# Longformer attention and a feed-forward layer on one core: the steady part's transfers in one written order, the global probabilities turned on VectorE and exchanged through HBM

## The chip, the cores and the metric

The kernel runs on one core of a Trainium2 chip. The metric is the device time of one execution in microseconds (us), and the figure to compare is the median of several runs. One execution was also profiled; its trace gives the time of each instruction on TensorE (PE for matmuls, PEld for weight loads), VectorE (DVE), ScalarE (ACT), GpSimd (POOL) and the sync engine's queue of transfers (SPq).

## The reference

Eight batches of eight heads: 512 local tokens per head attend to a window of 32 tokens on each side and to 32 global tokens; the 32 global tokens attend to everything. The result goes, token by token, through a layer of 512 x 2048, a leaky bend with a slope for each hidden unit, and a layer of 2048 x 512.

```python
s_g = scale * np.matmul(q_g, k_all.transpose(0, 1, 3, 2))
out_g = np.matmul(sm(s_g), v_all)
mask = np.abs(pos[:, None] - pos[None, :]) <= window
s_ll = np.where(mask, s_ll, -1000000000.0)
s_l = np.concatenate([s_lg, s_ll], axis=-1)
out_l = np.matmul(sm(s_l), np.concatenate([v_g, v_l], axis=2))
...
h = x @ w_in
g = np.maximum(h, 0.0) + alpha * np.minimum(h, 0.0)
return (g @ w_out).astype(np.float32)
```

## The kernel before

**Units of work.** Heads are taken in 32 pairs (P, four pairs to a batch). The feed-forward layers are cut into 16 tiles of 128 hidden units. A step t is one such tile for one group of tokens: `f1(t)` is the first layer's twelve matmuls into a PSUM bank `h_ps`, `leak` and `bend` make `g`, `round_g` and `rest_g` split it into a high and a low part (`gh`, `gl`), and `f2` adds it to four output banks in two parts, two steps later (`LAG = 2`). Groups are the eight batches and, last, all global tokens: 144 steps.

**Local attention of a pair.** `local_scores` (PSUM `s_ps`, from `qk`), maxima and exponentials (`p`), then the exchange that turns the probabilities: VectorE transposes 32 x 32 blocks (`pb`), one DMA writes them to HBM, and four DMAs a head read them back in another order (`pt`, `local_exchange`, `give` and `take`). `local_values` multiplies `pt` with `vw` into `o_ps`; `local_weights` scales the result (`xq`) and sends it through the same kind of exchange (`xb`) into `x_raw`, the input of the next group's first layer.

**Global attention of two pairs** (index k, sixteen in all). `global_scores` (PSUM `g_ps`, from `gn`; two short memsets fill an unused corner first), exponentials into `sg_sb`, `global_transposes` (four TensorE transposes into PSUM `gt`, copied by ScalarE and VectorE into `sgt_sb`; a rest of 32 columns is turned by VectorE), `global_values` (`go`, from `sgt_sb` and `vg`) and `global_outputs` (`gx`).

**What sets the order.** TensorE follows the order in which the code is written throughout. The first part, up to step 18, is spelled out in the string `ORDER` (lines 37 to 50): a letter for a function and a number for its pair or step, and it fixes ScalarE and VectorE too. After it comes the loop over steps (line 612), in which `plan` (lines 536 to 553) hangs local work on every fourth step and global work on chosen steps, at the places "mid" (ahead of the second layer's first part) or "post" (between its two parts). There ScalarE, VectorE and GpSimd are ordered by a scheduler. Transfers on SP keep the written order up to line 578, where `dma.on = False` hands them to the scheduler; only inside `local_exchange` are they kept in order. SP is one queue: a transfer that waits for its data holds all behind it.

**Buffers.** `vw` and `qk` have one buffer each for pairs from 4 on, so that a load can start only when TensorE has finished with the pair before. `g`, `gh`, `gl`, `p`, `pb`, `pt`, `xq` and `xb` share 21 buffers of 128 x 512. `h_ps`, `o_ps` and `go` share two PSUM banks, `s_ps`, `g_ps`, `gt` and `gx` two others.

Of the kernel before, what the change touches and what calls it, by code (L numbers as in the profile page):

```python
# [8 lines left out]
F32 = mybir.dt.float32  # L9
# [8 lines left out]
NB, NH, SL, SG, D = 8, 8, 512, 32, 64  # L18
NPAIR = 4
# [24 lines left out]
    x4 H7 L8 C5 L7 j10 V5 r9 T6 N5 k11 A7 g9 u10 j11 C6 X5 B7 x5 S7 H9 l10 k12 L9 F10 h12 R7 u11  # L44
    s12 V6 r10 l11 E7 A8 N6 g10 B8 j12 H10 S8 h13 F11 L10 k13 R8 u12 X6 r11 A9 x6 l12 E8 g11 T7
    s13 B9 j13 F12 h14 s14 u13 A10 k14 l13 r12 B10 H11 g12 F13 h15 L11 j14 C7 V7 r13 g13 u14 A11
    N7 k15 l14 X7 B11 s15 x7 H13 F14 H12 j15 A12 L12 u15 r14 l15 B12 g14 F15 d8 e8 L13 A13 r15 H14
    g15 H15 B13 L15 L14 F16 r16 g16 H16 L16 A14 V8 S9 B14 N8 R9 F17 p9 r17 q9 g17 d9 A15 B15 e9 H17
    L17 F18 r18 g18 G0 H18 L18 A16 B16
"""  # L50
GROUPS = [("l", b) for b in range(NB)] + [("g", 0)]
# [33 lines left out]
def longformer_ffn(ctx: ExitStack, tc: tile.TileContext, qk, vs, gn, vg, w, alpha, out):  # L85
# [13 lines left out]
    beta_sb = const.tile([128, NF], F32, name="beta_sb")  # L99
    pick = const.tile([128, 64], F32, name="pick")  # L100
    og_sb = const.tile([128, 128], F32, name="og_sb")
    sgt_sb = const.tile([128, 5, 2, 64], F32, name="sgt_sb")
    x_raw = const.tile([128, NPAIR, SL], F32, name="x_raw")
    x_glb = const.tile([128, NPAIR, NB * SG], F32, name="x_glb")

# [2 lines left out]
    def matmul(*a, **k):  # L108
        return tc.keep_in_program_order(nc.tensor.matmul(*a, **k))  # L109

    def transpose(*a):
        return tc.keep_in_program_order(nc.tensor.transpose(*a))  # L112

    def stage(name, dtype=F32):
        return work.tile([128, 512], dtype, tag="st", name=name, bufs=NST)
# [4 lines left out]
    def copy(engine, dst, src):  # L120
        if engine == "a":
            act.copy(dst, src)
        else:
            vec.tensor_copy(dst, src)

    def bank(tag, name):
        return psum.tile([128, 512], F32, tag=tag, name=name, bufs=2 if tag in "hs" else 1)
# [91 lines left out]
    def load_v(P):  # L219
        if P < NPAIR:  # L220
            t = wpool.tile([128, 2048], F32, tag="w", name="vw")
        else:
            t = work.tile([128, 2048], F32, tag="v", name="vw", bufs=1)
        vws[P] = t.rearrange("k (e i d) -> k e i d", e=2, i=8)
        for e in range(2):
            off = (P * KS + 32 * e) * 128
            src = bass.AP(tensor=vs.tensor, offset=off, ap=[[128, 128], [96 * 128, 8], [1, 128]])
            dma.dma_start(vws[P][:, e], src)
# [35 lines left out]
    def local_exps(P, heads=(0, 1)):  # L264
        if 0 in heads:
            z_of[P] = small("z", 8)
        for h in heads:
            src, mn, scale = ps_of.pop((P, h))
            p = pr_of[P, h] = stage("p") if P < NRAW else pr_of[P, h]
            for i in range(4):  # L270
                k = 2 * i + h
                act.activation(p[:, 128 * i : 128 * i + 128], src[:, i], AF.Exp, bias=mn[:, i : i + 1], scale=scale, accum_out=z_of[P][:, k : k + 1])
        if 1 in heads:
            rz_of[P] = small("rz", 8)
            act.activation(rz_of[P], z_of.pop(P), AF.Copy, bias=1e-9)
# [23 lines left out]
            dma.dma_start(put[32 * b : 32 * b + 32].rearrange("k (w n) -> k w n", w=4), spread[:, b].rearrange("(w k) n -> k w n", w=4))  # L299

    def local_exchange(P, heads=(0, 1)):
        on, dma.on = dma.on, True
        for h in heads:
            ps_of[P, h] = give(pr_of.pop((P, h)), "pb")
        if 1 in heads:
            for h in range(2):
                pt_of[P, h] = stage("pt")
                take(pt_of[P, h], ps_of.pop((P, h)))
        dma.on = on

    xs = {}

# [43 lines left out]
        xh, xl = xs[0, P]  # L356
        vec.tensor_tensor(xl, ps_of.pop(P), xh.bitcast(F32), op=ALU.subtract)

    gns, vgs, sgs, gz = {}, {}, {}, {}
    big = []  # L360

    def load_gn(k):
        if not big:
            big.append(wpool.tile([128, 2048], F32, tag="w", name="gn"))
        for e in range(2):
            gns[2 * k + e] = big[0][:, 576 * e : 576 * e + 576]
            dma.dma_start(gns[2 * k + e], gn[2 * k + e])

    def load_vg(k):
        for P in (2 * k, 2 * k + 1):  # L370
            vgs[P] = wide("vg")[:, 0:640].rearrange("k (y d) -> k y d", y=5)
            dma.dma_start(vgs[P], vg[P])

    def global_scores(k):
        ss = [bank("s", "g_ps") for h in range(2)]
        for h in range(2):
            vec.memset(ss[h][64:128, 256:288], -3.0e38)
        for r, c0, n in ((0, 32, 288), (1, 320, 256)):
            for e in range(2):
                t = gns[2 * k + e]  # L380
                for h in range(2):
                    hs, q0 = slice(64 * h, 64 * h + 64), 64 * r + 32 * e
                    matmul(ss[h][q0 : q0 + 32, 0:n], t[hs, 0:32], t[hs, c0 : c0 + n], start=True, stop=True)
        for e in range(2):
            del gns[2 * k + e]
        m, z = small("gm", 4), small("gz", 16)
        sg_sb = sgs[k] = big[0][:, 1152:1728].rearrange("q (h n) -> q h n", h=2)
        for h in range(2):
            vec.tensor_reduce(m[:, h : h + 1], ss[h][:, 0:288], axis=AX.X, op=ALU.max)
        vec.tensor_scalar(m[:, 2:4], m[:, 0:2], -0.125, None, op0=ALU.mult)  # L390
        vec.tensor_copy(m[0:64, 0:2], m[64:128, 2:4])
        vec.tensor_tensor(m[0:64, 2:4], m[0:64, 2:4], m[0:64, 0:2], op=ALU.min)
        vec.tensor_copy(m[64:128, 2:4], m[0:64, 2:4])
        for h in range(2):
            act.activation(sg_sb[:, h], ss[h][:, 0:288], AF.Exp, bias=m[:, 2 + h : 3 + h], scale=0.125, accum_out=z[:, h : h + 1])
        vec.tensor_copy(z[0:64, 2:4], z[64:128, 0:2])
        vec.scalar_tensor_tensor(z[0:64, 2:4], z[0:64, 2:4], 1e-9, z[0:64, 0:2], op0=ALU.add, op1=ALU.add)
        vec.reciprocal(z[0:64, 2:4], z[0:64, 2:4])
        vec.tensor_copy(z[64:128, 2:4], z[0:64, 2:4])
        gz[k] = z  # L400

    def global_transposes(k):
        ps, sg_sb = bank("s", "gt"), sgs.pop(k)
        for h in range(2):
            for e in range(2):
                c = 256 * h + 128 * e
                transpose(ps[:, c : c + 128], sg_sb[:, h, 128 * e : 128 * e + 128], ident)
        for h in range(2):
            dst = sgt_sb[:, 0:4, h].rearrange("k (r e) n -> k r e n", r=2)
            copy("ad"[h], dst, ps[:, 256 * h : 256 * h + 256].rearrange("k (e r n) -> k r e n", e=2, r=2))  # L410
            for e in range(2):
                vec.transpose(sgt_sb[0:32, 4, h, 32 * e : 32 * e + 32], sg_sb[32 * e : 32 * e + 32, h, 256:288])

    def global_values(k):
        ps = bank("h", "go")
        for y in range(5):
            for h in range(2):
                for e in range(2):
                    q0 = 64 * h + 32 * e
                    matmul(ps[q0 : q0 + 32, 0:64], sgt_sb[:, y, h, 32 * e : 32 * e + 32], vgs[2 * k + e][:, y, 64 * h : 64 * h + 64], start=(y == 0), stop=(y == 4))  # L420
        for e in range(2):
            del vgs[2 * k + e]
        z = gz.pop(k)
        for h in range(2):
            hs = slice(64 * h, 64 * h + 64)
            act.activation(og_sb[hs, hs], ps[hs, 0:64], AF.Copy, scale=z[hs, 2 + h : 3 + h])
# [94 lines left out]
    def plan(t, where, fn, P):  # L521
        at.setdefault((t, where), []).append((fn, P))
# [22 lines left out]
    for k in range(NPR // 2):  # L545
        u, v = step[k], step[k + 1]
        if k:
            plan(u - 2, "mid", load_gn, k)
            plan(u, "mid", global_scores, k)
        plan(u + 1, "mid", load_vg, k)  # L550
        plan(v - 2, "mid", global_transposes, k)
        at.setdefault((v, "mid"), []).insert(0, (global_values, k))
        plan(v + 1, "mid", global_outputs, k)

    def attention(t, where):
        for fn, P in at.pop((t, where), ()):
# [22 lines left out]

    def first_scores(P, warm):  # L580
        local_scores(P, warm)
        if P > NRAW:
            load_v(P)
        if P >= NPAIR:
            load_qk(P + 1)

    def first_values(P, warm):
# [4 lines left out]
    def first_f1(T, warm):  # L592
        f1(T, warm, (lambda c: split_x(1, c)) if T == NF - 1 else None)
        if T == NF:
            load_gn(0)

    def first_join(f):
        join(f)
# [1 line left out]
            load_weights(f + 6)  # L600

    on_tensor = {"S": first_scores, "T": local_transposes, "V": first_values, "X": local_outputs, "F": first_f1, "A": lambda T, n: f2(T, 0, n), "B": lambda T, n: f2(T, 1, n)}
    others = {"R": local_maxima, "E": local_exps, "C": local_copies, "N": local_weights, "x": round_x, "y": rest_x, "D": local_exchange, "p": lambda P: local_exps(P, (0,)), "q": lambda P: local_exps(P, (1,)), "d": lambda P: local_exchange(P, (0,)), "e": lambda P: local_exchange(P, (1,)), "G": global_scores, "h": take_high, "k": take_low, "s": shift, "j": first_join, "u": upper, "l": lower, "r": leak, "g": bend, "H": round_g, "L": rest_g}
    for word in ORDER.split():
        word, _, warm = word.partition("*")
        if word[0] in on_tensor:
# [78 lines left out]
```

## Time and profile before

| | us |
|---|---|
| median of three runs | 911.14 |
| lowest and highest | 910.88, 911.96 |
| the profiled execution | 908.84 |
| its span, first to last instruction | 907.1 |
| mean granted TensorE clock | 0.994 of full speed |

The page gives each engine's busy time and its share of the span. A row of the timeline reads: start, length, engine, line, operation, output from inputs with shapes, and how many; in square brackets, how long the engine had been idle and what ended that. A row of the list of waits reads: who waited for whom, in total, how often, and the longest. A row of the issues of transfers ends with KB each and the median time from issue to landing.

### The profile page before, as it was taken

How to read it: one execution, taken by the hardware profiler on the slowest of the kernel's cores; microseconds unless marked ns; L12 is line 12 of the kernel's file. 1: busy time of each engine (PE TensorE's matmuls, PEld its weight loads, DVE VectorE, ACT ScalarE, POOL GpSimd, SP SyncE). 2: the span in 40 equal slices, each digit the busy share in tenths (PEclk: the TensorE clock that was granted, in tenths of full speed). 3: DMA queues.
4: the chain of work that ended last, by engine and by line, in shares of the span. 5: the costliest groups of instructions: out<-in, count | busy, mean ns of one | idle time of the engine just before them, and what ended most of it. 6: DMA issues, size and time to landing. Idle time of an engine off the chain costs nothing.

```text
span 907.1 us, 21212 instructions
## 1 busy us (share of the span) xinstructions
PE 889.9 (98%) x8704; PEld 718.6 (79%) x8704; DVE 439.0 (48%) x840; ACT 387.7 (43%) x1078; POOL 163.3 (18%) x158
## 2 busy tenths in 40 slices
PE   8889999999999999999999999999999999999998
PEld 4568787787878778877888788877887888888898
DVE  6899996455454444454354434554454323111311
ACT  5786783334443334443343344343343233222322
POOL 3000000211212122112111221122112222222221
PEclk9999999999999999999999999999999999999999
DMA  9994235565446543754546454664535320100000
GB/s 329 342 408 189 81 110 166 183 203 182 159 143 209 183 155 123 246 192 160 180 147 211 149 171 148 213 205 164 185 123 180 112 93 24 46 1 1 12 36 25
DMA packets 139953, 140.33 MB, mean 155 GB/s; under 512 B 9296, under 2 KB 112208, under 8 KB 137808
## 3 DMA queue, kind: packets, MB, share of 16 engines
q1 hardware_dynamic: 139568, 138.72, 45.6%
q8 instruction: 68, 1.11, 0.5%
q14 instruction: 29, 0.24, 0.1%
q10 hardware_dynamic: 288, 0.26, 0.1%
HBM read 111.16 MB, written 27.79 MB: 153 GB/s over the span
## 4 chain that ended last, share of the span: by engine, by line
PE 92%; DMA 3%; SPq 3%; DVE 2%; ACT 0%; issue 0%; DVEq 0%
PE o L109 41%; PE h_ps L109 40%; PE s_ps L109 4%; PE o_ps L109 3%; SPq L78 3%; DMA qk<-in_qk_dram 2%; PE go L109 1%; PE g_ps L109 1%; DMA ws<-in_w_dram 1%; DVE wt L78 1%; PE gt L112 1%; PE pt L112 0%; PE gx L109 0%; ACT wt L78 0%; DVE xl L78 0%
## 5 line engine op out<-in xcount | busy, mean ns | idle before, releaser
L109 PE MATMUL h_ps<-xh,wt 128*128 128x512 f32 (+1 forms) x1152 | 340.0, 378 | 0.0
L475 POOL TENSOR_TENSOR gl<-g,gh 128x512 fp32r<-128x512 f32 (+1 forms) x128 | 156.0, 1219 | 737.0 <-ACT gh L78 632.5
L109 PE MATMUL o<-gh,wt 128*128 128x512 f32 (+1 forms) x1152 | 277.7, 383 | 0.0
L78 DVE SCALAR_TENSOR_TENSOR g<-g,beta_sb,h_ps 128x512 f32<-128x512 f32 (+1 forms) x144 | 102.3, 711 | 317.5 <-ACT g L78 316.2
L109 PEld LDWEIGHTS h_ps<-xh,wt 128*128 128x128 f32 x1152 | 212.0, 188 | 41.9 <-DVE wt L78 0.4
L109 PEld LDWEIGHTS o<-gh,wt 128*128 128x128 f32 x1152 | 204.7, 188 | 44.2 <-issue 6.3
L109 PE MATMUL h_ps<-xl,wt 128*128 128x512 f32 (+1 forms) x576 | 217.7, 378 | 0.0
L78 ACT ACTIVATE g<-h_ps 128x512 f32<-128x512 f32 (+1 forms) x144 | 82.1, 571 | 263.0 <-PE h_ps L109 228.4
L109 PE MATMUL o<-gl,wt 128*128 128x512 f32 (+1 forms) x576 | 151.3, 384 | 0.2 <-DVE gl L78 0.2
L109 PEld LDWEIGHTS h_ps<-xl,wt 128*128 128x128 f32 x576 | 108.4, 188 | 20.0
L78 ACT CAST gh<-g 128x512 fp32r<-128x512 f32 (+1 forms) x144 | 85.7, 597 | 87.3 <-DVE g L78 81.9
L109 PEld LDWEIGHTS o<-gl,wt 128*128 128x128 f32 x576 | 102.9, 188 | 23.4 <-issue 4.4
L78 ACT ACTIVATE p<-p,mn 128x128 f32<-128x128 f32 x192 | 74.5, 390 | 103.3 <-DVE mn L78 70.8
L78 DVE STREAM_TRANSPOSE pb<-p 128x512 f32<-128x512 f32 x48 | 34.1, 711 | 44.0 <-ACT p L78 43.2
L109 PEld LDWEIGHTS o_ps<-vw,pt 128*32 128x32 f32 x2048 | 31.3, 112 | 13.9 <-issue 7.2
L78 DVE TENSOR_TENSOR xq<-o_ps,rz 128x512 f32<-128x512 f32 x32 | 22.1, 691 | 40.0 <-PE o_ps L109 39.2
L109 PE MATMUL s_ps<-qk 64*32 64x128 f32 x2048 | 37.8, 278 | 0.6 <-DMA qk<-in_qk_dram 0.6
L109 PE MATMUL o_ps<-vw,pt 128*32 128x64 f32 x2048 | 36.7, 224 | 1.6 <-DMA pt<-pb 1.6
L78 ACT ACTIVATION_READ_ACCUMULATOR p<-p,mn 128x1 f32 x192 | 36.0, 188 | 0.0
L109 PEld LDWEIGHTS s_ps<-qk 64*32 64x32 f32 x2048 | 29.1, 107 | 6.6 <-issue 2.5
L78 DVE TENSOR_REDUCE mn<-p 128x4 f32<-128x512 f32 x48 | 30.5, 660 | 0.1
L78 DVE SCALAR_TENSOR_TENSOR p<-s_ps,mask 128x512 f32<-128x512 f32 x48 | 30.2, 664 | 0.0
(83 smaller groups left out, 541.2 us busy)
## 6 DMA issues: line engine op xcount, KB each, us to landing
vw<-in_vs_dram SPq DMA_DIRECT2D x64, 512.0 KB, 5.3
qk<-in_qk_dram SPq DMA_DIRECT2D x32, 672.0 KB, 6.6
ws<-in_w_dram SPq DMA_DIRECT2D x16, 1024.0 KB, 9.6
pb<-pb SPq DMA_DIRECT2D x48, 256.0 KB, 2.3
pt<-pb SPq DMA_DIRECT2D x192, 64.0 KB, 2.0
vg<-in_vg_dram SPq DMA_DIRECT2D x32, 320.0 KB, 3.5
gn<-in_gn_dram SPq DMA_DIRECT2D x32, 288.0 KB, 4.4
out_dram<-ost SPq DMA_DIRECT2D x32, 256.0 KB, 3.4
```

Of the source, the lines that this page charges most:

```text
L78: ins = call(*a, **k)
L109: return tc.keep_in_program_order(nc.tensor.matmul(*a, **k))
L112: return tc.keep_in_program_order(nc.tensor.transpose(*a))
L475: (vec if T < NF else nc.gpsimd).tensor_tensor(gl[:, 0:n], gs.pop(T)[:, 0:n], gh_of[T][:, 0:n].bitcast(F32), op=ALU.subtract)
```

## The change

Four things change.

1. `global_transposes` no longer uses TensorE. VectorE turns 32 x 32 blocks into a stage buffer (`sgb`), one DMA writes it to HBM, and four DMAs bring it back into `sgt_sb`. The copies from PSUM go. `global_values` reads `sgt_sb` in the new layout.
2. In the steady part all transfers on SP stand in written order: `local_exchange` switches the keeping of order on and nothing switches it off. The loads of `vw` and `qk` therefore stand behind the exchange of the pair before.
3. The global steps are planned anew: `global_fill` (the two memsets) is a function of its own and comes half a step earlier, `global_transposes`, `load_vg` and the next `load_gn` come one step after the scores.
4. In `ORDER` the exchange of pair 8 (`d8 e8`) moves ahead of `g14 F15`, and `f0` (`global_fill(0)`) stands ahead of `H17`.

```diff
-    N7 k15 l14 X7 B11 s15 x7 H13 F14 H12 j15 A12 L12 u15 r14 l15 B12 g14 F15 d8 e8 L13 A13 r15 H14
+    N7 k15 l14 X7 B11 s15 x7 H13 F14 H12 j15 A12 L12 u15 r14 l15 B12 d8 e8 g14 F15 L13 A13 r15 H14
-    g15 H15 B13 L15 L14 F16 r16 g16 H16 L16 A14 V8 S9 B14 N8 R9 F17 p9 r17 q9 g17 d9 A15 B15 e9 H17
+    g15 H15 B13 L15 L14 F16 r16 g16 H16 L16 A14 V8 S9 B14 N8 R9 F17 p9 r17 q9 g17 d9 A15 B15 e9 f0 H17
...
     def local_exchange(P, heads=(0, 1)):
-        on, dma.on = dma.on, True
+        dma.on = True
...
-        dma.on = on
...
+    def global_fill(k):
+        gps[k] = [bank("s", "g_ps") for h in range(2)]
+        for h in range(2):
+            vec.memset(gps[k][h][64:128, 256:288], -3.0e38)
+
     def global_scores(k):
-        ss = [bank("s", "g_ps") for h in range(2)]
-        for h in range(2):
-            vec.memset(ss[h][64:128, 256:288], -3.0e38)
+        ss = gps.pop(k)
...
     def global_transposes(k):
-        ps, sg_sb = bank("s", "gt"), sgs.pop(k)
+        sg_sb, blk = sgs.pop(k), stage("sgb")
+        for h in range(2):
+            dst = blk.rearrange("k (b h c n) -> k h c b n", b=4, h=2, c=2)[:, h]
+            vec.transpose(dst, sg_sb[:, h, 0:256].rearrange("q (c b n) -> q c b n", c=2, b=4))
         for h in range(2):
             for e in range(2):
-                c = 256 * h + 128 * e
-                transpose(ps[:, c : c + 128], sg_sb[:, h, 128 * e : 128 * e + 128], ident)
-        for h in range(2):
-            dst = sgt_sb[:, 0:4, h].rearrange("k (r e) n -> k r e n", r=2)
-            copy("ad"[h], dst, ps[:, 256 * h : 256 * h + 256].rearrange("k (e r n) -> k r e n", e=2, r=2))
-            for e in range(2):
-                vec.transpose(sgt_sb[0:32, 4, h, 32 * e : 32 * e + 32], sg_sb[32 * e : 32 * e + 32, h, 256:288])
+                vec.transpose(sgt_rest[0:32, h, 32 * e : 32 * e + 32], sg_sb[32 * e : 32 * e + 32, h, 256:288])
+        spread = dram.tile([128, 4, 128], F32, tag="sgb", name="sgb", bufs=2)
+        dma.dma_start(spread, blk.rearrange("k (b n) -> k b n", b=4))
+        for b in range(4):
+            dma.dma_start(sgt_main[32 * b : 32 * b + 32].rearrange("k (w n) -> k w n", w=4), spread[:, b].rearrange("(w k) n -> k w n", w=4))
...
         if k:
-            plan(u - 2, "mid", load_gn, k)
+            plan(u - 1, "post", global_fill, k)
             plan(u, "mid", global_scores, k)
+        plan(u + 1, "mid", global_transposes, k)
         plan(u + 1, "mid", load_vg, k)
-        plan(v - 2, "mid", global_transposes, k)
+        if k + 1 < NPR // 2:
+            plan(u + 1, "mid", load_gn, k + 1)
         at.setdefault((v, "mid"), []).insert(0, (global_values, k))
-        plan(v + 1, "mid", global_outputs, k)
+        at.setdefault((v + 1, "mid"), []).insert(0, (global_outputs, k))
...
     def first_scores(P, warm):
         local_scores(P, warm)
-        if P > NRAW:
-            load_v(P)
-        if P >= NPAIR:
+        if NPAIR <= P <= NRAW:
             load_qk(P + 1)
...
         if T == NF:
             load_gn(0)
+        if T == NF + 2:
+            load_v(NRAW + 1)
+            load_qk(NRAW + 2)
```

The queue of SP, one period of four steps in the steady part, before. The names are the transfer's target and source; `vw`, `qk`, `vg` and `gn` are loads, `xb` and `pb` go to HBM, `x_raw` and `pt` come back.

```order
L78 DMA vw<-in_vs_dram 128x8x128 x2
L78 DMA xb<-xb 128x512
L78 DMA qk<-in_qk_dram 128x1344
L78 DMA x_raw<-xb 32x4x128 x4
L78 DMA pb<-pb 128x512 x2
L78 DMA pt<-pb 32x4x128 x8
L78 DMA vg<-in_vg_dram 128x640 x2
L78 DMA gn<-in_gn_dram 128x576 x2
```

The same period of SP with the change, from the same point, the end of a pair's values.

```order
L78 DMA xb<-xb 128x512
L78 DMA x_raw<-xb 32x4x128 x4
L78 DMA pb<-pb 128x512 x2
L78 DMA pt<-pb 32x4x128 x8
L78 DMA vw<-in_vs_dram 128x8x128 x2
L78 DMA qk<-in_qk_dram 128x1344
L78 DMA sgb<-sgb 128x512
L78 DMA sgt_sb<-sgb 32x4x128 x4
L78 DMA vg<-in_vg_dram 128x640 x2
L78 DMA gn<-in_gn_dram 128x576 x2
```

Both exchanges of the pair now stand ahead of the loads of the next one, and the exchange of the global probabilities behind them.

VectorE in the first part before, around the exchange of pair 8 (`pb`), the splitting of group 1's input (`xl`) and one bend (`g`).

```order
L78 TENSOR_TENSOR wt<-wt 128x2x512
L78 SCALAR_TENSOR_TENSOR g<-g,beta_sb,h_ps 128x512
L78 TENSOR_TENSOR xl<-x_raw,xh 128x512 x4
L78 STREAM_TRANSPOSE pb<-p 128x4x4x32 x2
L78 TENSOR_TENSOR gl<-g,gh 128x512
```

VectorE at the same place with the change.

```order
L78 TENSOR_TENSOR wt<-wt 128x2x512
L78 STREAM_TRANSPOSE pb<-p 128x4x4x32 x2
L78 SCALAR_TENSOR_TENSOR g<-g,beta_sb,h_ps 128x512
L78 TENSOR_TENSOR xl<-x_raw,xh 128x512 x4
L78 TENSOR_TENSOR gl<-g,gh 128x512
```

The two transposes for pair 8 moved ahead of the bend and of the four splits; what stands behind `gl` is as before.

VectorE a little later before, from the second half of pair 9's exchange to the first global maxima (`gm`).

```order
L78 STREAM_TRANSPOSE pb<-p 128x4x4x32
L78 SCALAR_TENSOR_TENSOR g<-g,beta_sb,h_ps 128x512
L78 MEMSET g_ps 64x32 x2
L78 TENSOR_REDUCE gm<-g_ps 128x1 x2
L78 TENSOR_SCALAR gm<-gm 128x2
```

VectorE at the same place with the change.

```order
L78 STREAM_TRANSPOSE pb<-p 128x4x4x32
L78 MEMSET g_ps 64x32 x2
L78 SCALAR_TENSOR_TENSOR g<-g,beta_sb,h_ps 128x512
L78 TENSOR_REDUCE gm<-g_ps 128x1 x2
L78 TENSOR_SCALAR gm<-gm 128x2
```

The memsets, for which the global scores wait, moved ahead of the bend. On TensorE nothing moves: the sixteen rows `gt` go and every other row stands where it stood.

More of the change, by code (lines that the diff above doesn't have):

```diff
@@ L101, in longformer_ffn @@
     og_sb = const.tile([128, 128], F32, name="og_sb")
-    sgt_sb = const.tile([128, 5, 2, 64], F32, name="sgt_sb")
+    sgt_sb = const.tile([128, 640], F32, name="sgt_sb")
+    sgt_main = sgt_sb[:, 0:512]
+    sgt_cut = sgt_main.rearrange("k (r e h c n) -> k r e h c n", r=2, e=2, h=2, c=2)
+    sgt_rest = sgt_sb[:, 512:640].rearrange("k (h n) -> k h n", h=2)
     x_raw = const.tile([128, NPAIR, SL], F32, name="x_raw")
@@ L357, in rest_x @@
         vec.tensor_tensor(xl, ps_of.pop(P), xh.bitcast(F32), op=ALU.subtract)
-    gns, vgs, sgs, gz = {}, {}, {}, {}
+    gns, vgs, sgs, gz, gps = {}, {}, {}, {}, {}
     big = []
@@ L419, in global_values @@
                     q0 = 64 * h + 32 * e
-                    matmul(ps[q0 : q0 + 32, 0:64], sgt_sb[:, y, h, 32 * e : 32 * e + 32], vgs[2 * k + e][:, y, 64 * h : 64 * h + 64], start=(y == 0), stop=(y == 4))
+                    wt = sgt_cut[:, y // 2, e, h, y % 2] if y < 4 else sgt_rest[:, h, 32 * e : 32 * e + 32]
+                    matmul(ps[q0 : q0 + 32, 0:64], wt, vgs[2 * k + e][:, y, 64 * h : 64 * h + 64], start=(y == 0), stop=(y == 4))
         for e in range(2):
@@ L602, in longformer_ffn @@
     on_tensor = {"S": first_scores, "T": local_transposes, "V": first_values, "X": local_outputs, "F": first_f1, "A": lambda T, n: f2(T, 0, n), "B": lambda T, n: f2(T, 1, n)}
-    others = {"R": local_maxima, "E": local_exps, "C": local_copies, "N": local_weights, "x": round_x, "y": rest_x, "D": local_exchange, "p": lambda P: local_exps(P, (0,)), "q": lambda P: local_exps(P, (1,)), "d": lambda P: local_exchange(P, (0,)), "e": lambda P: local_exchange(P, (1,)), "G": global_scores, "h": take_high, "k": take_low, "s": shift, "j": first_join, "u": upper, "l": lower, "r": leak, "g": bend, "H": round_g, "L": rest_g}
+    others = {"R": local_maxima, "E": local_exps, "C": local_copies, "N": local_weights, "x": round_x, "y": rest_x, "D": local_exchange, "p": lambda P: local_exps(P, (0,)), "q": lambda P: local_exps(P, (1,)), "d": lambda P: local_exchange(P, (0,)), "e": lambda P: local_exchange(P, (1,)), "f": global_fill, "G": global_scores, "h": take_high, "k": take_low, "s": shift, "j": first_join, "u": upper, "l": lower, "r": leak, "g": bend, "H": round_g, "L": rest_g}
     for word in ORDER.split():
```

## The prediction

> **What bounds the kernel now.** I read the page's first two parts, then the busy time by stage, then the waits of TensorE, then the timeline around each wait. In the stage rows the number behind each engine's name in the heading is its busy time in that stretch.
>
> ```profile
> span 907.1 us, 21212 instructions
> ...
> PE 889.9 (98%) x8704; PEld 718.6 (79%) x8704; DVE 439.0 (48%) x840; ACT 387.7 (43%) x1078; POOL 163.3 (18%) x158
> ...
> core 0: us, PE busy (x) PEld busy (x) DVE busy (x) ACT busy (x) POOL busy (x), PEclk, DMA share, GB/s
> 0.00:60.00 60.00, 49.98 (x859) 31.60 (x860) 47.60 (x74) 41.62 (x118) 7.27 (x30) 0.91 0.99 357
> 60.00:170.00 110.00, 106.53 (x968) 85.31 (x967) 93.64 (x135) 74.18 (x166) 2.55 (x2) 1.00 0.49 168
> 170.00:810.00 640.00, 640.00 (x6289) 516.66 (x6288) 279.55 (x601) 246.42 (x739) 131.33 (x102) 1.00 0.47 154
> ...
> PE g_ps L109 <- DVE g_ps L78: 1.7, 1, 1.7
> PE o_ps L109 <- DMA pt<-pb: 1.6, 1, 1.6
> ```
>
> TensorE is the bound. From 170 to 810 us it is busy for 640.00 of 640.00 us at a granted clock of 1.00, so there the time changes only if work leaves TensorE or a wait arrives there. The transfers have room (share 0.47). Between 60 and 170 us TensorE lacks 110.00 - 106.53 = 3.47 us, and the two waits above are nearly all of it. Before 60 us neither the code nor the order of transfers changes. The change can therefore gain in two ways, the transposes it takes off TensorE and these two waits, and it can lose in one: by making TensorE wait in the steady part.
>
> **The transposes that leave TensorE.** Sixteen groups of four (gt) go.
>
> ```profile
> L112 PE MATMUL gt<-ident,gn x64: 270/272/273, 178.1 to 718.9; 128*128 128x128 f32 x64
> ...
> 230.56 0.39 PE L109 MATMUL h_ps<-xl,wt 128*128 128x512 f32 x1
> ...
> 235.84 0.39 PE L109 MATMUL h_ps<-xh,wt 128*128 128x512 f32 x1
> ...
> 254.66 0.39 PE L109 MATMUL h_ps<-xl,wt 128*128 128x512 f32 x1
> 254.89 0.60 PE L112 MATMUL gt<-ident,gn 128*128 128x128 f32 x4
> ...
> 260.43 0.62 PE L109 MATMUL h_ps<-xh,wt 128*128 128x512 f32 x2
> ```
>
> Both stretches are the same local step (second-layer matmuls, local values, local scores, the rest of the second layer), from the last first-layer matmul of one step to the first of the next. At 230 us no gt stands in it, at 254 us one does: 235.84 - 230.56 = 5.28 us against 260.43 - 254.66 = 5.77 us. All sixteen groups stand at such a place, so the gain is 16 x 0.49 = **7.8 us**. The listed durations overlap their neighbours and would give 64 x 0.272 = 17.4 us, which is the price of a rival below. In place of gt, VectorE transposes 32x32 blocks and five DMAs a group carry them through HBM; none of that is on TensorE.
>
> The Trainium skill's page "VectorE: DVE Perf Modes" (sections "The three transpose paths" and "Rules for kernel authors") speaks against this: it gives VectorE only 32x32 blocks and sends a full 128x128 transpose to TensorE where a PSUM destination will do. By that rule the change buys nothing; it looks at the time of one transpose, and the rows of this case show TensorE full and VectorE half idle, so I go by the rows.
>
> **The two waits of the head.**
>
> ```profile
> 139.56 1.23 DVE L78 TENSOR_TENSOR wt<-wt 128x1024 fp32r<-128x1024 f32 x1 [0.52 <-ACT wt L78]
> 140.70 0.74 DVE L78 SCALAR_TENSOR_TENSOR g<-g,beta_sb,h_ps 128x512 f32<-128x512 f32 x1
> 141.36 2.49 DVE L78 TENSOR_TENSOR xl<-x_raw,xh 128x512 fp32r<-128x512 f32 x4
> 143.77 1.30 DVE L78 STREAM_TRANSPOSE pb<-p 128x512 f32<-128x512 f32 x2
> ...
> 146.56 5.09 SPq L78 DMA_DIRECT2D pt<-pb  x8
> ...
> 146.73 0.62 PE L109 MATMUL h_ps<-xh,wt 128*128 128x512 f32 x2
> ...
> 151.35 0.32 PE L109 MATMUL o_ps<-vw,pt 128*32 128x64 f32 x8
> 153.27 0.99 PE L109 MATMUL o_ps<-vw,pt 128*32 128x64 f32 x56 [1.60 <-DMA pt<-pb]
> ...
> 162.85 0.71 DVE L78 STREAM_TRANSPOSE pb<-p 128x512 f32<-128x512 f32 x1
> 165.31 0.75 DVE L78 SCALAR_TENSOR_TENSOR g<-g,beta_sb,h_ps 128x512 f32<-128x512 f32 x1 [1.75 <-ACT g L78]
> 166.06 0.12 DVE L78 MEMSET g_ps<- 64x32 f32 x2
> ...
> 166.29 0.81 PE L109 MATMUL g_ps<-gn 64*32 64x288 f32 x16 [1.66 <-DVE g_ps L78]
> ```
>
> The exchange of pair 8 now stands ahead of g and of xl: its transposes can start when wt ends, at 140.75 instead of 143.77, 3.0 us sooner. The last pt lands at 153.27 - 3.0 = 150.3, before local values want it at 151.4. Gain **1.6 us**, with 1.1 us to spare. What is late instead: g and the four xl move back by 1.3 us, to 145.1 at most; the first layer that reads xl begins at 146.73, and the gl behind them ends when it did, because the same instructions run before it.
>
> The second wait is a memset of 0.12 us that stands behind a g which itself waits 1.75 us for ScalarE. It now stands ahead of that g, straight behind pb, so it is done by 163.7, while TensorE would reach the global scores at 166.29 - 1.66 = 164.6. Gain **1.7 us**. Sum: 7.8 + 1.6 + 1.7 = **11.1 us**.
>
> **The transfers in their new order.** Here the loss would come. One period of the steady part before:
>
> ```profile
> 181.58 1.00 SPq L78 DMA_DIRECT2D vw<-in_vs_dram  x2
> 183.05 0.45 SPq L78 DMA_DIRECT2D xb<-xb  x1
> 183.59 0.64 SPq L78 DMA_DIRECT2D qk<-in_qk_dram  x1
> 189.21 1.86 SPq L78 DMA_DIRECT2D x_raw<-xb  x4
> 191.16 0.85 SPq L78 DMA_DIRECT2D pb<-pb  x2
> 193.38 4.84 SPq L78 DMA_DIRECT2D pt<-pb  x8
> ...
> 188.15 0.71 DVE L78 STREAM_TRANSPOSE pb<-p 128x512 f32<-128x512 f32 x1 [0.90 <-ACT p L78]
> ...
> 206.78 1.10 PE L109 MATMUL o_ps<-vw,pt 128*32 128x64 f32 x64
> ...
> vw<-in_vs_dram SPq DMA_DIRECT2D x64, 512.0 KB, 5.3
> qk<-in_qk_dram SPq DMA_DIRECT2D x32, 672.0 KB, 6.6
> pb<-pb SPq DMA_DIRECT2D x48, 256.0 KB, 2.3
> ```
>
> Before, vw and qk left at once and had over 20 us to land; now they leave behind the last pt. If the exchange became no faster at all, vw would start at 193.38 + 4.84 = 198.2, its second half 0.5 us later, and land 5.3 us after, at 204.0. TensorE wants it at 206.78 less 0.49, or 206.3: 2.3 us to spare. qk, issued about 1.5 us behind the first vw, would land at 198.2 + 1.5 + 6.6 = 206.3, and scores follow one block of 1.0 us after values, at 207.3. So the slow end is "just in time". The fast end: xb no longer queues behind vw. It took 189.21 - 183.05 = 6.2 us until x_raw could go, where a pb of the same size lands in 2.3 us, so x_raw goes some 3.5 us sooner, and pb is then held only by its own transposes (the second ends at 188.86 and now waits until 191.6). The last pt leaves about 2 to 3 us sooner, at 195.5. I take this end, as pb's own row prices it, with some 4 us to spare in a period of 26 us, and cost the reordering at **nothing**; it cannot gain either, as TensorE has no idle time there. The cover that hides it is the time from pt to the next values; gone, every late microsecond counts once in each of the 22 periods still to come.
>
> The first period is the tightest one: four output writes stand in it too, and vw of pair 9 used to be loaded ahead of that pair's exchange. The writes take 4 x 0.6 = 2.4 us of SP, about the 2.3 us that even the slow end had to spare. The bound is 0 to 2 us, and I take 0, as for the fast end.
>
> The new sgb rows add a wait on SP, behind which sgt_sb, vg, gn and the next xb, x_raw, pb and pt stand.
>
> ```profile
> 192.53 0.69 PE L109 MATMUL g_ps<-gn 64*32 64x288 f32 x16
> 196.58 0.49 ACT L78 ACTIVATE gn<-g_ps,gm 128x288 f32<-128x288 f32 x1
> 199.55 0.75 DVE L78 SCALAR_TENSOR_TENSOR g<-g,beta_sb,h_ps 128x512 f32<-128x512 f32 x1 [1.17 <-ACT g L78]
> ```
>
> The probabilities are ready at 197.1, but the sgb transposes stand behind this g, so they end at about 201.0. With 2.3 us for sgb to land and eight issues (sgt_sb, vg, gn) at pt's 4.84 / 8 = 0.6 us, SP is free at 208.1; the next xb is ready 1.5 us after the end of values (183.05 - 181.58), at 206.3 + 1.1 + 1.5 = 208.9. Should sgb queue behind qk as xb did behind vw (6.2 us), xb is 3 us late and the pt after it is back at the slow end. The global values want sgt_sb at about 218, a period after 192, and it lands by 212 either way. On VectorE each new transpose costs between 0.36 us (half of pb's 0.71 for half the columns; I take this) and 0.71 us, at most 32 x 0.71 = 23 us of an engine that idles for half the span. One g stands behind them, and TensorE wants its bank only two steps of 5.3 us or more later, so nothing of that reaches TensorE.
>
> **The rivals.**
> - *Loads land late* (the other side). If SP's one queue is held longer than I reckon (a sgb that waits, slow landings while output is written), vw or qk lands after TensorE wants it, in every period. Break-even is 11.1 / 22 = 0.5 us a period; 1 us late gives 22 - 11 = 11 us more than before, **922**. For it: the slow end above leaves 0 to 2 us. Against it: xb's delay behind vw is plain in the rows and goes. 5%.
> - *The head keeps its waits* in another form (the first vw late, g and xl late, another instruction ahead of the memset): only 7.8 us are gained, **903.3**. For it: margins of 1 us. 13%.
> - *Nothing is left*: the 7.8 us come back as small waits of TensorE for banks or sgt_sb at the sixteen global steps, about 0.5 us each and the head's as well: **911**. Against it: 6 us of room for sgt_sb, two steps for a bank. 5%. The rule of "VectorE: DVE Perf Modes" in the Trainium skill, above, would end here.
> - *A transpose costs its listed time* (17.4 us in place of 7.8): **890.4**. Against it: four of them take 0.60 us on the timeline, not 1.1, and the matmul behind starts 0.35 us after the first. The Trainium skill's page "TensorE: Matmul & The Clock Gate", section "Part 4: PE-mode transpose", gives about 275 ns for one and mostly access latency; the trace agrees with the duration (272 ns), and the timeline shows that it overlaps. 2%.
>
> **How the numbers follow.** The profiled execution lasted 908.84 us with a span of 907.1; the sum takes that span to 896.0 and the execution to 897.7. The runs shown have a median of 911.14 (910.88 to 911.96), 2.3 us above the profiled one, and I set the forecast against the median: 911.14 - 11.1 = **900.0**, with 75%. Below it nearly nothing is left to gain, as TensorE is full (0.2 us of the 3.47 remain), so the low end is 898.5, about the spread of the runs. The high end takes in the kept head waits and the first period's 2 us: 905.0. Outside lie the late loads, the nothing and the listed time, 12%. A measurement of this kernel can tell about 0.2% (1.8 us) from no change: faster 0.90, same 0.05, slower 0.05.
>
> **What would show it.** Right: no gt on TensorE; stage 170 to 810 still without idle time; neither wait in the list of TensorE's waits; the step at a former gt at 5.28 us; xb landing near 2.3 us. Wrong: a wait of local values or scores for vw or qk in every period, or of the global values for sgt_sb.

## The result and the profile after

| | before | changed |
|---|---|---|
| median of 20 runs, us | 909.22 | 916.45 |
| lowest and highest | 906.42, 913.69 | 911.91, 921.69 |
| profiled execution | 908.84 | 913.61 |
| its span | 907.1 | 911.8 |

The ratio is 1.0079, with a 95% interval of 1.0064 to 1.0094. The kernel became slower by 7 us, where 11 us of gain were forecast. Of the changed kernel, the busy time of the engines, the busy time by stage and TensorE's waits from 170 to 810 us (the same rows of before stand in the prediction; before, no wait stood in this stretch):

```profile
PE 881.9 (97%) x8632; PEld 713.3 (78%) x8640; DVE 442.0 (48%) x856; ACT 384.8 (42%) x1062; POOL 163.3 (18%) x158
...
60.00:170.00 110.00, 109.80 (x984) 88.16 (x983) 94.59 (x139) 74.00 (x167) 5.07 (x4) 1.00 0.45 149
170.00:810.00 640.00, 625.22 (x6175) 503.77 (x6175) 278.63 (x605) 239.80 (x716) 127.50 (x100) 0.99 0.53 169
...
PE s_ps L112 <- DMA qk<-in_qk_dram: 10.1, 9, 1.7
PE o_ps L112 <- DMA vw<-in_vs_dram: 2.9, 5, 0.9
...
PE o_ps L112 <- issue: 1.7, 2, 1.2
```

From 60 to 170 us TensorE is now busy for 109.80 of 110 us: both waits of the head are gone. TensorE as a whole works 8.0 us less than before (881.9 against 889.9). But in the steady part, where it was never idle before, it now lacks 640.00 - 625.22 = 14.8 us. The list names the cause: TensorE waits for the loads of `qk` (10.1 us) and `vw` (2.9 us); 1.7 us have no releaser in the profile ("issue"). The waits stand in 9 of the 22 local steps, at most three in a row.

The idle time is not the whole loss. From the first local values of the steady part to the last it takes 577.6 us (173.77 to 751.38), and 558.1 us (174.55 to 732.61) in the run below in which `sgb` is not sent and no load is late there. Of the 19.5 us between them 14.8 are idle time; in the other 4.7 TensorE counts as busy, with the same matmuls. The forecast span of 896.0 plus 14.8 gives 910.8, close to the 911.8 measured, but in part by luck: it leaves out these 4.7 us, and the run without `sgb`'s transfers has a span of 893.0, 3.0 us under the forecast.

Where the loads lose their time is read from the queue of SP, here from the end of one pair's exchange (vw) to the next (the last two rows):

```profile
190.63 2.03 SPq L78 DMA_DIRECT2D vw<-in_vs_dram  x2
192.76 0.59 SPq L78 DMA_DIRECT2D qk<-in_qk_dram  x1
194.36 0.34 SPq L78 DMA_DIRECT2D sgb<-sgb  x1
202.03 2.62 SPq L78 DMA_DIRECT2D sgt_sb<-sgb  x4
204.70 0.91 SPq L78 DMA_DIRECT2D vg<-in_vg_dram  x2
205.70 0.85 SPq L78 DMA_DIRECT2D gn<-in_gn_dram  x2
206.64 0.38 SPq L78 DMA_DIRECT2D xb<-xb  x1
211.78 1.76 SPq L78 DMA_DIRECT2D x_raw<-xb  x4
213.63 2.26 SPq L78 DMA_DIRECT2D pb<-pb  x2
217.22 3.65 SPq L78 DMA_DIRECT2D pt<-pb  x8
220.91 1.06 SPq L78 DMA_DIRECT2D vw<-in_vs_dram  x2
222.07 1.01 SPq L78 DMA_DIRECT2D qk<-in_qk_dram  x1
```

And the timelines of VectorE and TensorE around it:

```profile
193.57 0.76 DVE L78 STREAM_TRANSPOSE sgb<-gn 128x256 f32<-128x256 f32 x2
201.55 0.71 DVE L78 STREAM_TRANSPOSE xb<-xq 128x512 f32<-128x512 f32 x1
...
201.43 1.15 PE L112 MATMUL s_ps<-qk 64*32 64x128 f32 x64 [0.67 <-DMA qk<-in_qk_dram]
226.27 1.10 PE L112 MATMUL o_ps<-vw,pt 128*32 128x64 f32 x64
229.07 1.15 PE L112 MATMUL s_ps<-qk 64*32 64x128 f32 x64 [1.70 <-DMA qk<-in_qk_dram]
253.43 0.55 PE L112 MATMUL o_ps<-vw,pt 128*32 128x64 f32 x16 [1.23 <-issue]
254.79 0.98 PE L112 MATMUL o_ps<-vw,pt 128*32 128x64 f32 x48 [0.81 <-DMA vw<-in_vs_dram]
256.63 1.96 PE L112 MATMUL s_ps<-qk 64*32 64x128 f32 x64 [0.86 <-DMA qk<-in_qk_dram]
```

Read the queue as a chain in which each row waits for the one above or for its data:

- `sgb` leaves at 194.36, and the first read of it, for which SP waits, at 202.03, 7.7 us later: the write stands behind `vw` and `qk`, 1.7 MB that left just ahead of it. It lands 0.6 us after `qk`, whose landing starts the scores at 201.43; a period later it is 0.6 us again (229.65 and 229.07).
- `xb` is ready at 201.55 + 0.71 = 202.26, but behind the four reads, `vg` and `gn` it leaves at 206.64, **4.4 us late**.
- `x_raw` follows it by 5.1 us, where 2.3 us had been taken: `xb` now stands behind the 1.2 MB of `vg` and `gn`. **2.8 us.**
- From `pb` to the first `pt` it is 3.6 us, where an undisturbed exchange needs 2.1 (shown below): **1.5 us.** Nearly all of it is the issue of the two writes, 2.26 us in place of 0.85.

From the moment `xb` is ready to the first `pt` it takes 217.22 - 202.26 = 15.0 us. Before it was 10.4 us (193.38 - 183.02), and the prediction's fast end had 7.6. So `vw` and `qk`, which now stand behind `pt`, leave late, and when `qk` lands, 7.0 us after its issue (229.07 - 222.07), TensorE has waited 1.70 us for it. The three scores in a row wait 0.67, then 1.70, then, with the values ahead of them, 2.90 us (1.23 + 0.81 + 0.86).

This is the longest of the sixteen standstills. In nine of them `sgb` leaves 0.1 to 1.3 us after SP has issued `qk`, and its first read follows 4.7 to 7.7 us later. In the other seven it leaves 3.4 us or more after `qk`, and the read follows 2.0 to 3.0 us later, about as forecast. A batch has three global steps in its four periods, and behind the period without one, as from 253 to 279 us, the standstill is short again:

```profile
269.99 0.86 SPq L78 DMA_DIRECT2D qk<-in_qk_dram  x1
...
279.05 0.33 SPq L78 DMA_DIRECT2D sgb<-sgb  x1
281.06 1.75 SPq L78 DMA_DIRECT2D sgt_sb<-sgb  x4
```

By these rows late loads make the next standstill long, and a long standstill makes the next loads late; the run with every second standstill, below, bears on this.

### The profile page after: what moved, and what is told of

It is laid out like the page before. It is cut to its first block, busy times and chain, and to the rows that moved or that the text cites. A ratio compares the mean times of both kernels' runs of the same rounds, so it can differ in the third digit from the quotient of the medians.

```text
span 911.8 us, 21242 instructions
## 1 busy us (share of the span) xinstructions
PE 881.9 (97%) x8632; PEld 713.3 (78%) x8640; DVE 442.0 (48%) x856; ACT 384.8 (42%) x1062; POOL 163.3 (18%) x158
## 4 chain that ended last, share of the span: by engine, by line
PE 78%; DMA 11%; SPq 7%; DVE 2%; issue 1%; ACT 0%; DVEq 0%
PE o L112 36%; PE h_ps L112 35%; DMA qk<-in_qk_dram 8%; SPq L78 7%; PE s_ps L112 3%; PE o_ps L112 2%; DMA pb<-pb 1%; PE go L112 1%; PE g_ps L112 1%; DVE wt L78 1%; DMA sgb<-sgb 1%; DMA xb<-xb 0%; PE pt L115 0%; DVE gm L78 0%; PE gx L112 0%
```

## The experiments

Three accounts stood against each other.

- **A**: the loads are late since SP stands still for `sgb` and hands the delay on through `xb`, `pb` and `pt`. It has two readings: the standstill is enough by itself, or (A2) it needs the slow landing of `xb` behind `vg` and `gn` and the loads behind `pt` as well.
- **B**: the written order alone puts the loads too late, whatever `sgb` does.
- **C**: the added traffic (five transfers a global step) slows every landing.

Each run was timed in rounds beside the kernel before on the same chip. The diffs of the head alone and of gt left out are against the kernel before, those of the others against the changed kernel, where nothing else is said.

| run | median us (n) | ratio to before | 95% interval |
|---|---|---|---|
| global transposes back on TensorE | 905.55 (12) | 0.9965 | 0.9949 to 0.9980 |
| sgb not sent | 896.18 (5) | 0.9873 | 0.9856 to 0.9890 |
| reads of sgb behind xb | 896.61 (4) | 0.9877 | 0.9861 to 0.9893 |
| the head alone | 906.31 (12) | 0.9977 | 0.9962 to 0.9992 |
| gt left out of before | 901.56 (6) | 0.9917 | 0.9896 to 0.9938 |
| sgb behind vg and gn | 896.41 (5) | 0.9867 | 0.9849 to 0.9886 |
| loads first again | 896.76 (4) | 0.9856 | 0.9838 to 0.9874 |
| every second standstill | 897.64 (6) | 0.9892 | 0.9867 to 0.9918 |
| the changed kernel again | 918.38 (6) | 1.0103 | 1.0080 to 1.0125 |

**Global transposes back on TensorE**, the written order of the transfers kept:

```diff
     def global_transposes(k):
-        sg_sb, blk = sgs.pop(k), stage("sgb")
+        ps, sg_sb = bank("s", "gt"), sgs.pop(k)
...
-                vec.transpose(sgt_rest[0:32, h, 32 * e : 32 * e + 32], sg_sb[32 * e : 32 * e + 32, h, 256:288])
-        spread = dram.tile([128, 4, 128], F32, tag="sgb", name="sgb", bufs=2)
...
+                transpose(ps[:, c : c + 128], sg_sb[:, h, 128 * e : 128 * e + 128], ident)
...
-        plan(u + 1, "mid", global_transposes, k)
+        plan(v - 2, "mid", global_transposes, k)
```

> The written order of transfers alone, with the global transposes back on TensorE, so no sgb on SP. Theory A (SP stands still for sgb, which queues behind vw and qk; that makes xb, then pt, then the next vw and qk late): the loads land in time, the two head waits stay gone, ratio to before 0.9963 (3.3 of 909 us less), TensorE without idle time from 170 to 810 us. Theory B (loads that start only behind the last pt are too late by themselves): TensorE waits for qk and vw as in the changed kernel, some 15 us, ratio about 1.012. Theory C (the added traffic, wherever it stands in the queue): as theory A, 0.9963.

The busy time by stage of this run (stage, us, then TensorE's busy time):

```profile
170.00:800.00 630.00, 629.51 (x6243) 508.29 (x6242) 275.08 (x591) 243.42 (x732) 128.17 (x100) 1.00 0.48 159
```

In the steady part only 0.49 us of idle time are left, and the run gains what the head gains (3.0 us of 3.3). The written order by itself costs nothing: B falls.

**sgb not sent**: the write and the four reads go, so that the main part of `sgt_sb` is never filled and the global tokens' result lacks it; all work on VectorE and TensorE stays.

```diff
-        spread = dram.tile([128, 4, 128], F32, tag="sgb", name="sgb", bufs=2)
-        dma.dma_start(spread, blk.rearrange("k (b n) -> k b n", b=4))
-        for b in range(4):
-            dma.dma_start(sgt_main[32 * b : 32 * b + 32].rearrange("k (w n) -> k w n", w=4), spread[:, b].rearrange("(w k) n -> k w n", w=4))
```

> The changed kernel without the five transfers of sgb (VectorE still transposes; the first four fifths of sgt_sb stay zero, so the global tokens' result is left out in part). Theory A and theory C: no wait for vw or qk in the steady part, ratio 0.988 (11 us less than before). Theory B: waits as in the changed kernel, ratio about 1.004 to 1.008.

```profile
170.00:800.00 630.00, 630.00 (x6218) 509.23 (x6217) 282.31 (x607) 241.65 (x720) 129.93 (x102) 1.00 0.48 159
```

TensorE is full, and the run is 12.4 us faster than before. The whole loss hangs on the five transfers of `sgb`; A and C both allow that.

**Reads of sgb behind xb**: the same transfers, all of them, but the four reads go to SP behind the next `xb`, so that SP does not stand still for `sgb`.

```diff
-            take(x_raw[:, P % NPAIR], give(xq, "xb"))
+            spread = give(xq, "xb")
+            if pending:
+                global_take()
+            take(x_raw[:, P % NPAIR], spread)
...
         dma.dma_start(spread, blk.rearrange("k (b n) -> k b n", b=4))
+        pending.append(spread)
+
+    def global_take():
+        spread = pending.pop()
```

> The changed kernel with the same transfers, but the four reads of sgb stand behind the next xb, so that SP does not stand still between writing and reading sgb. Theory A: xb leaves when it is ready, the loads land in time, ratio 0.988 (898 us). Theory B: ratio 1.004 or more. Theory C: the traffic is the same, so the ratio stays about 1.008.

SP's queue in this run, over the same stretch:

```profile
196.63 0.34 SPq L78 DMA_DIRECT2D sgb<-sgb  x1
...
198.04 0.86 SPq L78 DMA_DIRECT2D gn<-in_gn_dram  x2
204.55 0.33 SPq L78 DMA_DIRECT2D xb<-xb  x1
204.97 2.31 SPq L78 DMA_DIRECT2D sgt_sb<-sgb  x4
207.64 1.73 SPq L78 DMA_DIRECT2D x_raw<-xb  x4
...
211.59 4.59 SPq L78 DMA_DIRECT2D pt<-pb  x8
...
203.82 0.71 DVE L78 STREAM_TRANSPOSE xb<-xq 128x512 f32<-128x512 f32 x1
```

`xb` leaves at 204.55, as soon as VectorE has it (203.82 + 0.71 = 204.53), and the first `pt` follows 7.1 us later instead of 15.0. No wait of TensorE for a load is left. The traffic is the same to the byte, so C falls. The run takes away more than the standstill, though: `vg` and `gn` now leave 6.5 us ahead of `xb` and are out of its way, so that it lands within 3.1 us. It can't tell the readings of A apart. This version beats both kernels, by 11.9 us against before.

**The head alone**: the kernel before with the change's string `ORDER` and `global_fill`, and nothing else.

```diff
-    N7 k15 l14 X7 B11 s15 x7 H13 F14 H12 j15 A12 L12 u15 r14 l15 B12 g14 F15 d8 e8 L13 A13 r15 H14
-    g15 H15 B13 L15 L14 F16 r16 g16 H16 L16 A14 V8 S9 B14 N8 R9 F17 p9 r17 q9 g17 d9 A15 B15 e9 H17
+    N7 k15 l14 X7 B11 s15 x7 H13 F14 H12 j15 A12 L12 u15 r14 l15 B12 d8 e8 g14 F15 L13 A13 r15 H14
+    g15 H15 B13 L15 L14 F16 r16 g16 H16 L16 A14 V8 S9 B14 N8 R9 F17 p9 r17 q9 g17 d9 A15 B15 e9 f0 H17
```

> The kernel before with only the two moves in ORDER (exchange of pair 8 earlier, first memsets ahead of the bend). All theories: both waits of 1.6 and 1.7 us go, ratio 0.9964 (3.3 us less). If they come back elsewhere, 1.000.

```profile
60.00:170.00 110.00, 109.68 (x983) 87.91 (x982) 96.10 (x140) 75.06 (x169) 3.86 (x3) 1.00 0.49 167
```

Both waits go (109.68 against 106.53 us busy, 3.15 us). The time falls by 2.2 us, and the interval (0.7 to 3.5 us) holds the forecast 3.3.

**gt left out of before**: the 64 transposes of TensorE and their copies out of PSUM go, so that the global probabilities are not turned and the global tokens' result is not the reference's.

```diff
-                transpose(ps[:, c : c + 128], sg_sb[:, h, 128 * e : 128 * e + 128], ident)
...
-            copy("ad"[h], dst, ps[:, 256 * h : 256 * h + 256].rearrange("k (e r n) -> k r e n", e=2, r=2))
```

> The kernel before without the 64 global transposes on TensorE and the copies of their result (four fifths of sgt_sb stay zero: this part of the global tokens' result is left out). If a group costs TensorE 0.49 us, 16 x 0.49 = 7.8 us less than before, ratio 0.9914; if each transpose costs its listed 0.272 us, 17.4 us less, ratio 0.981. The two head waits stay.

A ratio of 0.9917 of 909.64 is 7.5 us, with an interval from 5.6 to 9.5 us: the 16 x 0.49 = 7.8 us read from the distance of neighbouring matmuls, and not the 17.4 us of the listed durations.

**sgb behind vg and gn**: the loads of the global step are planned ahead of its transposes. SP still stands still for `sgb`, but `xb` no longer queues behind 1.2 MB of loads.

```diff
-        plan(u + 1, "mid", global_transposes, k)
         plan(u + 1, "mid", load_vg, k)
         if k + 1 < NPR // 2:
             plan(u + 1, "mid", load_gn, k + 1)
+        plan(u + 1, "mid", global_transposes, k)
```

> The changed kernel with vg and gn ahead of sgb and its reads, so that xb no longer queues behind 1.2 MB of vg and gn, while SP still stands still until sgb has landed. Theory A1 (standing still alone makes the loads late): sgb lands later still, waits for qk and vw stay, ratio 1.003 or more. Theory A2 (both parts are needed: SP's standing still, 4 us, and xb's slow landing behind vg and gn, 3 us): xb lands in about 2.3 us, the waits for qk and vw go or nearly go, ratio 0.988 to 0.993.

SP's queue of this run, with VectorE's `xb`:

```profile
198.66 0.40 SPq L78 DMA_DIRECT2D sgb<-sgb  x1
206.02 1.75 SPq L78 DMA_DIRECT2D sgt_sb<-sgb  x4
207.86 0.38 SPq L78 DMA_DIRECT2D xb<-xb  x1
210.05 1.73 SPq L78 DMA_DIRECT2D x_raw<-xb  x4
211.87 0.85 SPq L78 DMA_DIRECT2D pb<-pb  x2
214.00 4.40 SPq L78 DMA_DIRECT2D pt<-pb  x8
...
204.83 0.71 DVE L78 STREAM_TRANSPOSE xb<-xq 128x512 f32<-128x512 f32 x1
```

The standstill is as long as in the changed kernel (206.02 - 198.66 = 7.4 us; over the sixteen steps the median from issue to landing of `sgb` is 6.6 us, against 4.8 there), but `xb` lands in 2.2 us and `pt` follows `pb` by 2.1 us. From `xb` ready (205.54) to the first `pt` it is 8.5 us, and the loss is gone. So the standstill alone costs nothing here, and A holds in the reading A2: in the changed kernel it does its harm by pushing `vg` and `gn` to the place straight ahead of `xb`, as well as by its length.

**Loads first again**: `local_exchange` gives the order of transfers outside it back to the scheduler, as before the change; the scheduler puts `vw` and `qk` ahead of the exchange.

```diff
-        dma.on = True
+        on, dma.on = dma.on, True
...
+        dma.on = on
```

> The changed kernel with one part undone: outside local_exchange the scheduler orders SP again, so vw and qk stand ahead of xb and of pb as before, while sgb and its reads still make SP stand still. Theory A: SP's standing still has nothing urgent behind it, since the loads have 20 us to land; TensorE waits for no load, ratio 0.988. If standing still for sgb hurts by itself (a late pt, or a late sgt_sb), ratio 0.995 to 1.01 with TensorE waiting for pt or sgt_sb.

```profile
197.56 0.33 SPq L78 DMA_DIRECT2D sgb<-sgb  x1
201.20 1.75 SPq L78 DMA_DIRECT2D sgt_sb<-sgb  x4
204.01 1.03 SPq L78 DMA_DIRECT2D vw<-in_vs_dram  x2
...
215.35 4.82 SPq L78 DMA_DIRECT2D pt<-pb  x8
```

`vw` leaves 11 us ahead of the first `pt` and is in time whatever the exchange does. The run gains as much as the others. Behind `vg` and `gn` alone (1.2 MB) `sgb` lands within 3.6 us.

**Every second standstill**: the reads of `sgb` go behind `xb` at even global steps and stay where the change put them at odd ones. The diff is against the run with the reads behind xb.

```diff
         pending.append(spread)
+        if k % 2:
+            global_take()
```

> The changed kernel, with the four reads of sgb behind the next xb at every second global step (even k) and where the change put them at the others (odd k). If each standstill of the sync engine's queue costs its own period and no more, half of the loss stays: midway between 1.0079 and 0.9877, or 0.998. If the lateness of one period is handed on to the next, and a wait of TensorE comes of several in a row, then more than half goes: 0.992 or less, TensorE's waits for qk and vw together under 4 us instead of 14.

```profile
PE s_ps L112 <- DMA qk<-in_qk_dram: 3.0, 3, 1.5
...
170.00:800.00 630.00, 626.86 (x6202) 506.08 (x6201) 282.63 (x612) 241.18 (x720) 128.72 (x101) 1.00 0.54 174
```

Half of the standstills leave 3.1 of the 14.8 us of idle time, and the ratio's interval ends at 0.9918, well below the 0.998 of a cost for each by itself. So the lateness is handed on from period to period. The standstills that stay are themselves short: 2.0 to 2.8 us in seven of the eight and 6.2 in one, where the changed kernel has 4.7 us and more in nine of sixteen. That fits a standstill that is long only where late loads stand right ahead of it; no run holds the landing of `sgb` fixed and varies the rest.

**The changed kernel again**, on the chip of the run before it:

> The changed kernel as it is, beside the run before it on the same chip. If the loss belongs to the kernel and not to the chip on which it was first timed: 1.006 to 1.010 again, waits of TensorE for qk and vw of 10 to 18 us. If it belongs to that chip: near 0.988.

The loss is there again (1.0103), so it belongs to the kernel. The profiled run is slower than the first one (919.4 against 911.8 us of span) though the idle time in the steady part is about the same (14.1 against 14.8 us). From this profile, three stretches of 10 us (the granted clock is the third number from the end) and TensorE's timeline at two of these places; the last row is from the first profile:

```profile
250.00:260.00 10.00, 6.77 (x93) 5.22 (x99) 3.14 (x6) 2.69 (x5) 2.56 (x2) 0.84 0.66 207
260.00:270.00 10.00, 10.00 (x96) 8.11 (x84) 6.81 (x14) 5.34 (x21) 0.76 (x1) 0.82 0.34 116
360.00:370.00 10.00, 8.17 (x148) 6.27 (x147) 4.48 (x9) 1.57 (x4) 2.08 (x2) 0.83 0.63 203
...
256.65 0.67 PE L112 MATMUL o_ps<-vw,pt 128*32 128x64 f32 x16 [2.27 <-issue]
257.99 1.51 PE L112 MATMUL o_ps<-vw,pt 128*32 128x64 f32 x48 [0.67 <-DMA vw<-in_vs_dram]
259.80 1.96 PE L112 MATMUL s_ps<-qk 64*32 64x128 f32 x64 [0.30 <-DMA qk<-in_qk_dram]
...
365.83 1.80 PE L112 MATMUL s_ps<-qk 64*32 64x128 f32 x64 [0.94 <-DMA qk<-in_qk_dram]
...
469.02 1.15 PE L112 MATMUL s_ps<-qk 64*32 64x128 f32 x64 [1.13 <-DMA qk<-in_qk_dram]
```

After 2.27 us without work the values take 0.67 + 1.51 us instead of 1.10, and the scores 1.96 instead of 1.15. The granted clock was 0.84 and 0.82 there. From 170 to 750 us this profile has four such places, at 250, 360, 570 and 680 us, all right behind waits; the first profile has one, from 250 to 270 us (0.77 and 0.89). From the first local values of the steady part to the last it takes 581.6 us here (177.44 to 758.99), 23.5 more than without `sgb`'s transfers, so that 9.4 us count as busy beyond the idle time, against 4.7 in the first profile. The other 3.7 us between the two profiles stand ahead of the first of these values (177.44 against 173.77), where no load of the steady part is waited for; the granted clock of the first 60 us was 0.91 here and 1.00 in the first.

## Why the prediction was wrong

- **gt off TensorE, 7.8 us: right.** Leaving gt out of the kernel before gives 7.5 us. The rival with the listed time falls. So does the Trainium skill's rule in "VectorE: DVE Perf Modes" ("Rules for kernel authors") for this kernel: with the transfers in a better order, VectorE's way takes 11.9 us off the kernel together with the head.
- **The two waits of the head, 3.3 us: right in mechanism.** TensorE gained 3.15 us there by the stage; the median fell by 2.2 us, with 3.3 inside the interval.
- **The first period, 0 us: right.** No load is waited for in it; the first wait in the steady part is that at 201.43.
- **VectorE and the global values: right.** Two transposes of `sgb` take 0.76 us, 0.38 each against 0.36 estimated, and no wait for `sgt_sb` is among TensorE's waits.
- **"cost the reordering at nothing": the step that failed.** In it the chain from `xb` to `pt` was priced at the fast end. Its terms against the rows: `sgb`'s landing 2.3 us taken, 7.7 measured in the period shown and 4.8 in the median (the prediction had named 6.2 as the bad case, and stopped at "back at the slow end"); `xb`'s landing at the price of an undisturbed `pb`, 2.3 taken, 5.1 measured there and 4.2 in the median, because the reason why `xb` was slow before (1.0 MB of `vw` ahead of it) came back in another form (1.2 MB of `vg` and `gn`); `pb` to `pt` 1.5 us longer. The slow end was just in time with 1.0 us to spare, and all of these together lie beyond it.
- **Its error was to bound the delays one at a time.** Each bound was near the truth or harmless alone, as the runs show that keep the standstill and take away `xb`'s slow landing (0.9867) or the loads behind `pt` (0.9856). They act on one queue, one after the other, and there they add; and `sgb`'s landing depends on how late the loads ahead of it left, so that a late period makes the next one later. The prediction looked at one period by itself.
- **The rival "loads land late" came true**, with its own break-even: 14.8 us over 22 periods is 0.67 us each, above the 0.5 that it named, though the waits stand in 9 of the 22 and not in every one. From the median of before in this comparison, 909.22 - 11.1 + 14.8 = 912.9, 3.5 us below the 916.45 measured; the matmuls that took longer are of that size. The rival had 5%, with the argument that `xb`'s delay behind `vw` goes. That delay went, but its place was taken.
- **The clock was not in the sum.** The prediction took waits at their length. In the two profiles of the changed kernel 4.7 and 9.4 us of the loss lie beyond the idle time; the first shows a lower granted clock right behind waits at one place, the second at four. That the waits are the only cause of the lower clock was not tested. The time of the runs goes with their mean clock only loosely: 911.91 us at 1.000 and 921.69 at 0.987, but also 913.58 at 0.991 and 918.41 at 0.996.

## What to carry to other kernels

A write to HBM that is read back on the same queue had no fixed price here: 2.0 us with nothing close ahead of it, up to 7.7 right behind 1.7 MB of loads, and the queue stood still until it had landed. Before such a round trip is added, list what leaves in the microseconds ahead of it and what stands behind it, and add the worst cases along the queue up to the load that the bound engine waits for. Here it was enough to put the read behind the next write, by which time its data had landed: the same transfers in that order made 1.0079 into 0.9877.

## What the runs showed of the hardware that was not expected

A write of 256 KB landed in 2.2 us (`xb` in the run with `sgb` behind `vg` and `gn`), in 3.6 and 5.1 us behind 1.2 MB of loads (`sgb` with the loads first again, `xb` in the changed kernel), and in 7.7 us behind 1.7 MB (`sgb` in the changed kernel), with the share of the transfer engines' busy time at 0.53 over the steady part. The mean share says little about how long one small transfer waits.

A wait of TensorE of 1.70 us left the scores behind it at 1.15 us. Waits of 0.90 and 0.94 us close together (second profile, at 364 and 365 us) were followed by the same 64 matmuls in 1.80 us and a granted clock of 0.83. Waits of 0.51, 0.89 and 1.13 us close together (first profile, 465 to 469 us) were followed by 1.15 us and a clock of 1.00. So the lower clock stood behind groups of waits, but not behind every group: 1.84 us in all were enough once, 2.53 us were not another time. What decides was not tested. The Trainium skill's page "TensorE: Matmul & The Clock Gate", section "HAM oscillation — how this bites in real kernels", tells of a lower clock after idle gaps of more than about 3.4 us. These traces show the lower clock too, but no single wait in the steady part was longer than 2.27 us.
